# Attention scores over four PSUM banks, the last product of a step split around three down products, and later first values, in a fused attention and feed-forward kernel

## The chip, the cores and the metric

The kernel runs on one core of one Trainium2 chip. The metric is the device time of one execution in microseconds (us): the median of three timed runs was 1604.03 us before the change (1603.75, 1604.03 and 1604.44). A core has a matrix engine (PE, whose matmuls write to PSUM, a memory of eight banks of 512 float32 columns by 128 partitions), a vector engine (DVE), a scalar engine (ACT), GpSimd (POOL), and SyncE (SP), which here only issues transfers. Every engine works through its own list of instructions in order, and engines wait for each other through semaphores.

## The reference

```python
g = sigmoid((x * gate_w).sum(-1))
a = attention(x, wq, wk, wv, wo, beta)         # 32 heads of 18, four segments of 512 tokens
b = (gelu(x @ w_gate) * (x @ w_up)) @ w_down   # 576 -> 4608 -> 576
return g * a + (1 - g) * b

# attention, for each head and segment s, with a memory M, z carried from segment to segment:
p   = softmax(q @ k.T * scale + causal_mask)   # 512 x 512
o   = sigmoid(beta) * (phi(q) @ M) / (phi(q) @ z + 1e-6) + (1 - sigmoid(beta)) * (p @ v)
M  += phi(k).T @ v;   z += phi(k).sum()
```

The sequence has 2048 tokens of width 576. All inputs are float32. The kernel keeps float32 accuracy with float16 matmuls: each operand is split into a high and a low float16 word, and three products (high·high, high·low, low·high) are summed in PSUM.

## The kernel before, in words

A first stage (to about 227 us) projects queries, keys and values and builds the memory term. The stage that the change touches follows: 72 **steps** (`step(v)`, v = 0 to 71), one for each pair of a slice of 128 hidden columns (f = v // 2) and a half of the tokens. A step does three kinds of work, interleaved in an order that the program writes out by hand for PE, ACT, DVE and POOL; only SP's list is ordered by the build.

- **Gate and up.** Gate and up products of two token blocks are formed from seven sub-products of six 512-column matmuls each (`product`), plus single matmuls for the last 64 rows (`rest`, `low_rests`). They accumulate in the PSUM banks V, G (called X in the code) and U (called Y). DVE copies or adds between them: L1138 copies the first sum out of V, L1141 copies G to U, L1177 copies U out, L1196 and L1203 (the g1 and g0 additions) add U and V to what was copied, ACT applies GELU, and at the beginning of the next step `end_pair` runs L1021 (`hidden`), which multiplies by the up product in G and in U. The sub-product named S4 is the last one of a step and adds to U, which the g1 addition must have read before.
- **Down.** From step 4 on, eight down products a step (`down`: six 288-column matmuls, L999) go to the two PSUM banks `dn`, in turn, and DVE adds each to the accumulator (L1007, the eviction). Five of them are called early (`early`, spread over the step), three late.
- **Attention.** From step 2 to 65 two score blocks a step, an even one in the middle and an odd one at the end. `scores` issues four matmuls, one for each block of 128 queries, with 128, 256, 384 and 512 keys (causal). They use 54 rows of the array, either from row 0 or from row 64, and two that lie in different row halves run side by side. DVE adds the mask and takes the maximum of each piece (L910, one custom instruction and a tiny read of its accumulator; `put` in `step`), which also frees the bank. ACT forms exponentials and a float16 pair, POOL the low word, SP transposes it by DMA (L940), and one step later `values` (L954, 40 matmuls of 37 columns for a head's block pair, 20 for each block) multiplies by v into the bank `pv`; `normalize` reads it.

A step of steady state lasts 18.4 to 18.5 us. Steps 0 to 3 have no down products; the first heads' values are issued at the end of steps 3 and 4 (`values(2 * k - 2)` for v <= 4) and at the beginning of steps 4 and 5. From step 69 on, `finish` also splits the output projection's weights: L108 on ACT, L111 on DVE. Behind step 71 come the last down products and the output projection.

Of the kernel before, what the change touches and what calls it, by code (L numbers as in the profile page):

```python
# [13 lines left out]
OP = mybir.AluOpType  # L14
# [4 lines left out]
P = 128  # L19
# [3 lines left out]
DH = 18  # L23
L = 512
# [18 lines left out]
def kernel(ctx: ExitStack, tc: tile.TileContext, xs, wqk, wv, wo, wgu, wd, beta, out):  # L43
# [803 lines left out]
    with tc.tile_pool(name="keep", bufs=2, side="right", reuse_waits="tile") as kp, ExitStack() as tail:  # L847
# [40 lines left out]
        PIECES = (((3,), 0), ((2, 0), 64), ((1,), 0))  # L888

        def scores(a):  # L890
# [6 lines left out]
            for qis, r in PIECES:  # L897
                o = bank("dn", 2) if qis == (1,) else bank("st", 2)
                spots, off, h = [], 0, slice(r, r + 3 * DH)
                for qi in qis:  # L900
                    n = (qi + 1) * P
                    pe.matmul(o[:, off : off + n], q[h, e * L + qi * P : e * L + (qi + 1) * P],  # L902
                              kt[h, e * L : e * L + n], start=True, stop=True)
                    spots.append((qi, o[:, off : off + n]))
                    off += n
                put.append(spots)

            def piece(i):
                for qi, ov in put[i]:
                    dve.tensor_tensor_reduce(prob[a][:, COL[qi] : COL[qi + 1]], ov, mask[:, L - (qi + 1) * P :],  # L910
                                             1.0, -3e38, OP.add, OP.max, mx[a][:, qi : qi + 1])
# [122 lines left out]
        def product(o, f, a, x, h, l, start=False):  # L1034

            w = pair_g[f]
            for k in range(2):
# [72 lines left out]
        def end_pair():  # L1110

            for g in ends:
                hidden(*g)
            for f, c, o, g in ends:
                hidden_pair(f, c, g)
            ends.clear()

        def step(v):
# [19 lines left out]
            dve.tensor_copy(g1, V)  # L1138
# [11 lines left out]
            put(2 * k - 1, 2)  # L1150
            puts.pop(2 * k - 1, None)
            if on(k - 2):
                values(2 * k - 3)
# [31 lines left out]
            if on(k - 2):  # L1185
# [8 lines left out]
            if on(k):  # L1194
                puts[2 * k] = scores(2 * k)
# [152 lines left out]
```

## Time and profile before

| | |
|---|---|
| median of three runs | 1604.03 us (1603.75 to 1604.44) |
| the profiled execution's own time | 1603.76 us |
| its span from the first to the last instruction | 1602.0 us |
| PE busy | 1593.6 us, 99% of the span |
| DVE, ACT, POOL busy | 71%, 73%, 71% |
| granted PE clock | full speed in all slices |
| PE's waits that the trace lists, all entries together | 5.0 us |

A row of a timeline gives start, duration, engine, source line, operation, the program's names of output and inputs, shape, how many instructions are merged in it, and in brackets the idle time of the engine ahead of it with what ended it. A matmul's duration includes the time in which its result drains, so the next one starts well before its end: six 512-column matmuls in a row start 0.215 us apart while each is listed with 0.379 us. An idle time in brackets is counted from the listed end, so it is some 0.16 us shorter than the delay of the start. Times per step are read from the starts.

### The profile page before, as it was taken

How to read it: one execution, taken by the hardware profiler on the slowest of the kernel's cores; microseconds unless marked ns; L12 is line 12 of the kernel's file. 1: busy time of each engine (PE TensorE's matmuls, PEld its weight loads, DVE VectorE, ACT ScalarE, POOL GpSimd, SP SyncE). 2: the span in 40 equal slices, each digit the busy share in tenths (PEclk: the TensorE clock that was granted, in tenths of full speed). 3: DMA queues.
4: the chain of work that ended last, by engine and by line, in shares of the span. 5: the costliest groups of instructions: out<-in, count | busy, mean ns of one | idle time of the engine just before them, and what ended most of it. 6: DMA issues, size and time to landing. Idle time of an engine off the chain costs nothing.

```text
span 1602.0 us, 32613 instructions
## 1 busy us (share of the span) xinstructions
PE 1593.6 (99%) x11924; PEld 932.9 (58%) x11924; DVE 1142.2 (71%) x2938; ACT 1162.6 (73%) x1968; POOL 1136.7 (71%) x1093
## 2 busy tenths in 40 slices
PE   9999999999999999999999999999999999999999
PEld 6655754555555555555555555555555555555577
DVE  6575785777777777777777777777777777766643
ACT  6666446888888888888888888888888888864200
POOL 2233647898878888888979788888879797785300
PEclk9999999999999999999999999999999999999999
DMA  6532344788879788878887897988788788846251
GB/s 246 189 123 80 135 145 99 118 136 124 144 114 143 124 141 123 145 135 126 142 128 132 130 144 125 143 128 143 133 136 137 133 135 128 128 74 154 61 133 60
DMA packets 472016, 209.00 MB, mean 130 GB/s; under 512 B 427568, under 2 KB 437040, under 8 KB 471344
## 3 DMA queue, kind: packets, MB, share of 16 engines
q1 hardware_dynamic: 471856, 206.92, 70.9%
q8 instruction: 94, 1.54, 0.4%
q14 instruction: 66, 0.54, 0.1%
HBM read 90.99 MB, written 27.26 MB: 74 GB/s over the span
## 4 chain that ended last, share of the span: by engine, by line
PE 94%; ACT 2%; DMA 1%; DVE 1%; SPq 1%; issue 0%; DVEq 0%
PE dn L999 26%; PE U L1039 17%; PE V L1039 12%; PE G L1039 11%; PE pv L954 4%; PE st L328 3%; PE st L318 2%; PE U L1046 2%; PE dn L328 2%; PE st L902 2%; PE G L318 1%; PE V L1051 1%; PE G L1051 1%; PE U L318 1%; PE V L1046 1%; PE G L1046 1%
## 5 line engine op out<-in xcount | busy, mean ns | idle before, releaser
L934 POOL TENSOR_TENSOR ph<-pf,ph 128x512 f16<-128x512 f32 (+1 forms) x256 | 354.3, 1406 | 176.6 <-ACT ph L933 176.6
L999 PE MATMUL dn<-paird,hh 128*128 128x288 f16 x3396 | 476.5, 286 | 0.3 <-DVE acc L1007 0.3
L1039 PEld LDWEIGHTS <-pairg 128*128 128x128 f16 x3024 | 285.0, 98 | 308.7 <-issue 13.2
L999 PEld LDWEIGHTS <-hh 128*128 128x128 f16 x3456 | 332.3, 98 | 137.8 <-issue 2.3
L1007 DVE SCALAR_TENSOR_TENSOR acc<-dn,ev,acc 128x288 f32<-128x288 f32 x534 | 274.0, 516 | 94.4 <-PE dn L999 85.6
L923 ACT ACTIVATE pf<-pf,mb,esc 128x512 f32<-128x512 f32 (+3 forms) x512 | 293.0, 642 | 6.7
L1039 PE MATMUL G<-x,pairg 128*128 128x512 f16 x864 | 209.9, 379 | 0.3 <-DVE gl L1021 0.3
L1039 PE MATMUL U<-xt,pairg 128*128 128x512 f16 x864 | 210.0, 379 | 0.0
L1026 POOL TENSOR_TENSOR hh<-gl,hh 128x512 f16<-128x512 f32 x144 | 164.0, 1161 | 45.0 <-ACT hh L1025 45.0
L910 DVE CUSTOM_DVE_ANT_0 pf<-st,mask 128x512 f32<-128x512 f32 (+2 forms) x384 | 184.0, 505 | 0.0
L299 POOL TENSOR_TENSOR pairg<-raw,pairg 128x640 f16<-128x640 f32 (+2 forms) x144 | 174.1, 1231 | 12.3 <-ACT pairg L295 12.3
L933 ACT ACTIVATE ph<-pf 128x512 f16<-128x512 f32 (+1 forms) x256 | 172.4, 720 | 0.0
L1177 DVE COPY gl<-U 128x512 f32<-128x512 f32 x72 | 49.8, 691 | 130.2 <-PE U L1039 130.2
L295 ACT ACTIVATE pairg<-raw 128x640 f16<-128x640 f32 (+2 forms) x144 | 89.5, 648 | 68.4 <-POOL raw L289 38.9
L264 POOL TENSOR_SCALAR raw<-raw,sc 128x640 f32<-128x640 f32 x72 | 135.0, 1888 | 0.0
L1029 ACT ACTIVATE gl<-gl,sc 128x512 f32<-128x512 f32 x144 | 98.2, 717 | 42.4 <-DVE gl L1196 25.0
L1196 DVE TENSOR_TENSOR gl<-U,gl 128x512 f32<-128x512 f32 x72 | 49.8, 691 | 79.9 <-PE U L1051 72.6
L1039 PE MATMUL V<-xt,pairg 128*128 128x512 f16 x432 | 105.7, 381 | 0.0
L1039 PE MATMUL U<-x,pairg 128*128 128x512 f16 x432 | 105.0, 379 | 0.4 <-DVE gl L1196 0.4
L1039 PE MATMUL V<-x,pairg 128*128 128x512 f16 x432 | 104.8, 378 | 0.4 <-ACT hh L1025 0.2
L1025 ACT ACTIVATE hh<-gl 128x512 f16<-128x512 f32 x144 | 82.9, 616 | 26.2 <-DVE gl L1021 26.0
L920 ACT ACTIVATE mb<-mx,esc 128x4 f32<-128x4 f32 x128 | 37.8, 295 | 85.6 <-DVE mx L910 83.0
(268 smaller groups left out, 2569.9 us busy)
## 6 DMA issues: line engine op xcount, KB each, us to landing
raw<-in_wgu_dram SPq DMA_DIRECT2D x36, 640.0 KB
rawd<-in_wd_dram SPq DMA_DIRECT2D x36, 288.0 KB
qk<-stage SPq DMA_DIRECT2D x36, 256.0 KB
qt<-qk SPq DMA_DIRECT2D x128, 72.0 KB
kt<-qk SPq DMA_DIRECT2D x128, 72.0 KB
vp<-vstage SPq DMA_DIRECT2D x16, 296.0 KB
vt<-vp SPq DMA_DIRECT2D x16, 296.0 KB
qt<-qk SPq DMA_DIRECT2D x128, 36.0 KB
```

The source lines that it names most:

```text
L264: pool.tensor_scalar(r, r, scl[f // 2][0][:, 0:1], None, OP.mult)
L295: act.activation(spot(f, *p, 0), raw_g[f][:, p[0] : p[1]], AF.Copy)
L299: pool.tensor_tensor(spot(f, *p, 1), raw_g[f][:, p[0] : p[1]], spot(f, *p, 0), OP.subtract)
L910: dve.tensor_tensor_reduce(prob[a][:, COL[qi] : COL[qi + 1]], ov, mask[:, L - (qi + 1) * P :], 1.0, -3e38, OP.add, OP.max, mx[a][:, qi : q ...
L923: act.activation(r, r, AF.Exp, bias=b[:, qi : qi + 1], scale=esc[:, 0, c : c + 1])
L933: act.activation(h[:, 0, cols], p[:, cols], AF.Copy)
L934: pool.tensor_tensor(h[:, 1, cols], p[:, cols], h[:, 0, cols], OP.subtract)
L999: pe.matmul(o[:, :NH], hh[:, a, q * P : (q + 1) * P], w[:, b, n * NH : (n + 1) * NH], start=i == 0, stop=i == 5)
L1007: dve.scalar_tensor_tensor(av, o[:, :NH], ev, av, OP.mult, OP.add)
L1026: pool.tensor_tensor(hh[:, 1], t, hh[:, 0], OP.subtract)
L1029: act.activation(t, o, AF.Gelu_apprx_tanh, scale=scl[f // 2][0][:, 2 + c : 3 + c])
L1039: pe.matmul(o, w[:, i, (a + k) * P : (a + k + 1) * P], x[:, b + k], start=start and k == 0 and i == 0 and b == h, stop=k == 1 and i == 1, ...
```

## The change

The four score matmuls are issued in the order 512, 384, 256, 128 keys instead of 512, 384, 128, 256, with the row halves as before (0, 64, 64, 0), so the 256-key block moves to the second half and the 128-key block to the first. The 128-key block no longer shares the 384-key block's bank: it takes a `dn` bank, so a score block holds both `st` banks and both `dn` banks.

The DVE work on the pieces moves with it. Of an even block, the two pieces in `dn` come directly behind the scores, ahead of the two additions g1 and g0; the two in `st` stay between evictions. Of an odd block, the pieces in `dn` come between the two `hidden` of the next step, and the two in `st` keep their place.

S4 is issued in two halves of three matmuls, with the three late downs between them. The rest of G (U4) moves from behind product A12 to behind the values in the middle of the step. In steps 4 and 5 values are issued half a step later: blocks 0 and 1 at the beginning and in the middle of step 4, 2 and 3 at the beginning of step 5, 4 in its middle. `normalize(0)` moves to the end of step 4. In steps 1 to 3 the copy out of V comes ahead of `end_pair`. The split of the output weights moves behind the place of `normalize`.

```diff
-        PIECES = (((3,), 0), ((2, 0), 64), ((1,), 0))
+        PIECES = ((3, 0), (2, 64), (1, 64), (0, 0))
...
-            for qis, r in PIECES:
-                o = bank("dn", 2) if qis == (1,) else bank("st", 2)
...
+            for i, (qi, r) in enumerate(PIECES):
+                h, n = slice(r, r + 3 * DH), (qi + 1) * P
+                o = bank("st" if i < 2 else "dn", 2)[:, :n]
...
-        def product(o, f, a, x, h, l, start=False):
+        def product(o, f, a, x, h, l, start=False, ks=(0, 1)):
...
-        def end_pair():
+        def end_pair(between=()):
-            for g in ends:
+            for i, g in enumerate(ends):
                 hidden(*g)
+                if i == 0:
+                    for put in between:
+                        put()
...
+            first, middle = {3: ((), ()), 4: ((0,), (1,)), 5: ((2, 3), (4,))}.get(
+                v, ((2 * k - 3,) * on(k - 2), (2 * k - 2,) * on(k - 1)))
-            end_pair()
-            act_squares(v)
-            V = ahead.pop(v) if v in ahead else first_product(v)
-            g1 = gl_tile()
-            dve.tensor_copy(g1, V)
+            if v in ahead:
+                V, g1 = ahead.pop(v), gl_tile()
+                dve.tensor_copy(g1, V)
+                end_pair()
+                act_squares(v)
+            else:
+                end_pair([lambda i=i: put(2 * k - 1, i) for i in (2, 3)])
+                act_squares(v)
+                V, g1 = first_product(v), gl_tile()
+                dve.tensor_copy(g1, V)
...
-            if on(k - 2):
-                values(2 * k - 3)
+            for a in first:
+                values(a)
...
+            if v >= LAST + 2:
+                finish_pairs(v - LAST)
             product(X, f, A12, x1, 2, 6)
-            rest(X, f, U4, x1, (0,) if fb else (0, 1))
+            if not fb:
+                rest(X, f, U4, x1)
...
             if on(k):
                 puts[2 * k] = scores(2 * k)
+            put(2 * k, 2)
+            put(2 * k, 3)
             dve.tensor_tensor(g1, Y, g1, OP.add)
             gelu(f, e, g1, g1)
-            put(2 * k, 2)
...
-            if on(k - 1) and v > 4:
-                values(2 * k - 2)
+            for a in middle:
+                values(a)
+            if fb:
+                rest(X, f, U4, x1, (0,))
...
-            product(Y, f, S4, x2_, 2, 6)
-            rest(Y, f, UG, x2_, (0,) if fb else (0, 1))
+            product(Y, f, S4, x2_, 2, 6, ks=(0,))
             some(fb - 1, late[:1])
             if low is not None:
                 result_low(low)
             some(fb - 1, late[1:])
-            if on(k - 1) and v <= 4:
-                values(2 * k - 2)
+            if v == 4:
+                normalize(0)
+            product(Y, f, S4, x2_, 2, 6, ks=(1,))
+            rest(Y, f, UG, x2_, (0,) if fb else (0, 1))
```

No instruction is added or removed on PE, DVE, ACT or POOL; they move. In the lists of the changed kernel the lines have other numbers: L900 is the score matmul (L902 before), L906 the mask and maximum (L910), L1003 the eviction (L1007), L1017 `hidden` (L1021), L1144 the copy out of V (L1138), L1147 the copy of G to U (L1141), L1209 and L1215 the g1 and g0 additions (L1196 and L1203).

The first place is PE's list at a score block, here the four score matmuls and the first matmul behind an odd block. Before:

```order
L902 LDWEIGHTS qt
L902 MATMUL st<-kt,qt 128x512
L902 LDWEIGHTS qt
L902 MATMUL st<-kt,qt 128x384
L902 LDWEIGHTS qt
L902 MATMUL st<-kt,qt 128x128
L902 LDWEIGHTS qt
L902 MATMUL dn<-kt,qt 128x256
```

And of the change:

```order
L900 LDWEIGHTS qt
L900 MATMUL st<-kt,qt 128x512
L900 LDWEIGHTS qt
L900 MATMUL st<-kt,qt 128x384
L900 LDWEIGHTS qt
L900 MATMUL dn<-kt,qt 128x256
L900 LDWEIGHTS qt
L900 MATMUL dn<-kt,qt 128x128
```

The third matmul is now the 256-key one, in row half 64 behind the 384-key one, and the fourth is the 128-key one, in row half 0 behind the 512-key one; both go to `dn`.

The second place is DVE's list from the even scores of a step to its first late down, whose eviction is the row that follows in both. Before:

```order
L1196 TENSOR_TENSOR gl<-U,gl 128x512
L910 ISA pf,mx<-dn,mask 128x256
L910 ISA mx 128x1
L1203 TENSOR_TENSOR gl<-V,gl 128x512
L1007 SCALAR_TENSOR_TENSOR acc<-dn,ev,acc 128x288
L910 ISA pf,mx<-st,mask 128x512
L910 ISA mx 128x1
L1007 SCALAR_TENSOR_TENSOR acc<-dn,ev,acc 128x288
L910 ISA pf,mx<-st,mask 128x384
L910 ISA mx 128x1
L910 ISA pf,mx<-st,mask 128x128
L910 ISA mx 128x1
```

Of the change:

```order
L906 ISA pf,mx<-dn,mask 128x256
L906 ISA mx 128x1
L906 ISA pf,mx<-dn,mask 128x128
L906 ISA mx 128x1
L1209 TENSOR_TENSOR gl<-U,gl 128x512
L1215 TENSOR_TENSOR gl<-V,gl 128x512
L1003 SCALAR_TENSOR_TENSOR acc<-dn,ev,acc 128x288
L906 ISA pf,mx<-st,mask 128x512
L906 ISA mx 128x1
L1003 SCALAR_TENSOR_TENSOR acc<-dn,ev,acc 128x288
L906 ISA pf,mx<-st,mask 128x384
L906 ISA mx 128x1
```

Both pieces in `dn` now stand ahead of the two additions, and the list begins with an instruction that waits for the scores, where it began with one that waits for U.

The third place is DVE's list at the border of two steps, from the first `hidden` to the copy of G to U. Before:

```order
L1021 SCALAR_TENSOR_TENSOR gl<-G,sc,gl 128x512
L1021 SCALAR_TENSOR_TENSOR gl<-U,sc,gl 128x512
L1138 COPY gl<-V 128x512
L910 ISA pf,mx<-st,mask 128x512
L910 ISA mx 128x1
L1141 COPY U<-G 128x512
```

And of the change:

```order
L1017 SCALAR_TENSOR_TENSOR gl<-G,sc,gl 128x512
L906 ISA pf,mx<-dn,mask 128x256
L906 ISA mx 128x1
L906 ISA pf,mx<-dn,mask 128x128
L906 ISA mx 128x1
L1017 SCALAR_TENSOR_TENSOR gl<-U,sc,gl 128x512
L1144 COPY gl<-V 128x512
L906 ISA pf,mx<-st,mask 128x512
L906 ISA mx 128x1
L1147 COPY U<-G 128x512
```

The two pieces in `dn` have moved in behind the first `hidden`, so the second one, the copy out of V and the copy of G to U stand behind two more instructions.

More of the change, by code (lines that the diff above doesn't have):

```diff
@@ L1032, in gl_tile @@
             return mp2.tile([P, L], F32, name="gl", bufs=3)
-        def product(o, f, a, x, h, l, start=False):
+        def product(o, f, a, x, h, l, start=False, ks=(0, 1)):
             w = pair_g[f]
-            for k in range(2):
+            for k in ks:
                 for i, b in ((0, h), (0, l), (1, h)):
@@ L1149, in step @@
             put(2 * k - 1, 1)
[L1150 removed]
+            if v < 4:
+                put(2 * k - 1, 2)
+                put(2 * k - 1, 3)
             puts.pop(2 * k - 1, None)
[L1152 to L1153 removed]
+            for a in first:
+                values(a)
             weights_first(fb, i4)
```

20 lines of the change are left out of this document (8 added, 12 removed).

## The prediction

> **What bounds the kernel now.** I read the page first, for the engine that is never idle, then the chain that ended last, then the timelines of PE and DVE through a step of the steady state, then PE's rows that carry an idle time.
>
> ```profile
> PE 1593.6 (99%) x11924; PEld 932.9 (58%) x11924; DVE 1142.2 (71%) x2938; ACT 1162.6 (73%) x1968; POOL 1136.7 (71%) x1093
> PE 94%; ACT 2%; DMA 1%; DVE 1%; SPq 1%; issue 0%; DVEq 0%
> ```
>
> PE works through 99% of the span and carries 94% of the chain. So time comes out only where PE's matmuls get shorter or run side by side, or where one of its few waits goes; and a wait of PE that is new costs its full length. One step (its middle to its end), on PE:
>
> ```profile
> 802.72 0.38 PE L1046 MATMUL U<-x,pairg 128*128 128x512 f16 x1
> 803.03 0.39 PE L1051 MATMUL U<-x,pairg 64*128 64x512 f16 x1
> 803.25 0.38 PE L902 MATMUL st<-kt,qt 54*128 54x512 f16 x3
> 803.48 0.27 PE L902 MATMUL dn<-kt,qt 54*128 54x256 f16 x1
> 803.67 0.67 PE L954 MATMUL pv<-vt,pt 128*128 128x37 f16 x20
> 804.19 1.63 PE L999 MATMUL dn<-paird,hh 128*128 128x288 f16 x12
> 805.66 1.46 PE L1039 MATMUL U<-x,pairg 128*128 128x512 f16 x6
> 806.95 0.38 PE L1046 MATMUL U<-x,pairg 128*128 128x512 f16 x1
> 807.17 2.40 PE L999 MATMUL dn<-paird,hh 128*128 128x288 f16 x18
> 809.50 0.39 PE L1051 MATMUL G<-x,pairg 64*128 64x512 f16 x1
> ```
>
> By the starts: a score block takes 0.42, values 0.52, a down product 0.735 (1.47 for two), a sub-product of six 1.29, a single 512-column matmul 0.22, and a change from 128 rows to 64 adds 0.09 (0.31 instead of 0.22). Three late downs take 2.33 - 0.09 = 2.24 where 3 x 0.735 = 2.20: PE waits some 0.04 in the third, which takes the bank of the first. DVE in the same stretch:
>
> ```profile
> 803.46 0.69 DVE L1196 TENSOR_TENSOR gl<-U,gl 128x512 f32<-128x512 f32 x1 [1.32 <-PE U L1051]
> 804.07 0.41 DVE L910 CUSTOM_DVE_ANT_0 pf<-dn,mask 128x256 f32<-128x256 f32 x1
> 804.41 0.69 DVE L1203 TENSOR_TENSOR gl<-V,gl 128x512 f32<-128x512 f32 x1
> 805.12 0.52 DVE L1007 SCALAR_TENSOR_TENSOR acc<-dn,ev,acc 128x288 f32<-128x288 f32 x1
> 805.56 0.68 DVE L910 CUSTOM_DVE_ANT_0 pf<-st,mask 128x512 f32<-128x512 f32 x1
> 806.16 0.51 DVE L1007 SCALAR_TENSOR_TENSOR acc<-dn,ev,acc 128x288 f32<-128x288 f32 x1
> 806.60 0.54 DVE L910 CUSTOM_DVE_ANT_0 pf<-st,mask 128x384 f32<-128x384 f32 x1
> 807.07 0.28 DVE L910 CUSTOM_DVE_ANT_0 pf<-st,mask 128x128 f32<-128x128 f32 x1
> 807.28 0.08 DVE L910 DVE_READ_ACCUMULATOR2_ANT mx<- 128x1 f32 x1
> 808.10 0.52 DVE L1007 SCALAR_TENSOR_TENSOR acc<-dn,ev,acc 128x288 f32<-128x288 f32 x1 [0.74 <-PE dn L999]
> ```
>
> The last row is the eviction of the first late down: it ends at 808.62, and the third late down starts at 809.50 - 0.09 - 0.735 = 808.67, so the release of a bank reaches PE 0.05 after the eviction's end. DVE had waited 0.74 before it, so the wait of 0.04 is the bare turn-round of two banks.
>
> **Part 1, the score block: shorter.** The pieces by shape:
>
> ```profile
> L902 PE MATMUL st<-kt,qt 54*128 54x384 f16 x128 | 41.5, 325 | 0.0
> L902 PE MATMUL dn<-kt,qt 54*128 54x256 f16 x128 | 34.2, 267 | 0.0
> L902 PE MATMUL st<-kt,qt 54*128 54x128 f16 x128 | 27.3, 213 | 0.0
> ```
>
> 128 columns more cost 0.054 (267 against 213 ns). Row half 0 now streams 512 + 256 columns and half 64 streams 384 + 128, that is 768 against 512; after the change both stream 640. The block ends up to 128 columns = 0.054 earlier; bounds 0 (the halves do not overlap in the second pair) and 0.054. The last piece starts 0.23 after the first, which is one 512-column stream (0.22), so the halves overlap now; I take 0.05. Each step of 62 (4 to 65) has two blocks: -0.10 a step.
>
> **Part 2, what that meets: DVE ahead of the third late down.** S4 is halved, so the late downs start 0.65 + 0.22 earlier; U4 (0.22) now lies before the early ones. Counted from the start s of the even scores, the first late down starts at 0.37 + 0.52 + 0.215 + 1.47 + 0.645 = s+3.22, and the third, with its old wait, at 3.22 + 1.51 = s+4.73.
>
> DVE's list now begins with the 256-key piece. That matmul starts when the 384-key one has streamed, 325 - 213 + 54 = 0.166 after s, and ends 0.267 later, at s+0.44. After it come, start to start: 0.34 (256-key piece), 0.21 (128), g1, g0, 0.44 (eviction), 0.60 (512), 0.44, 0.47 (384), then the eviction of the first late down (0.52) and 0.05. g1 followed by g0, and g0 by an eviction that need not wait, stand in a step without scores:
>
> ```profile
> 1463.69 0.69 DVE L1196 TENSOR_TENSOR gl<-U,gl 128x512 f32<-128x512 f32 x1 [1.32 <-PE U L1051]
> 1464.30 0.68 DVE L1203 TENSOR_TENSOR gl<-V,gl 128x512 f32<-128x512 f32 x1
> 1464.89 0.94 DVE L1007 SCALAR_TENSOR_TENSOR acc<-dn,ev,acc 128x288 f32<-128x288 f32 x2
> ```
>
> 0.61 and 0.59. The sum is 4.27. How long the custom instruction takes to start once its matmul has ended is not in the trace, since it never waits. The nearest rows: an addition starts 0.04 after (803.03 + 0.39 = 803.42, then 803.46), a copy 0.10 after:
>
> ```profile
> 810.15 1.47 PE L1039 MATMUL V<-xt,pairg 128*128 128x512 f16 x6
> 811.72 0.69 DVE L1138 COPY gl<-V 128x512 f32<-128x512 f32 x1 [0.21 <-PE V L1039]
> ```
>
> With 0.04 the third late down starts at 0.44 + 0.04 + 4.27 = s+4.75, some 0.02 to 0.03 later than with its old wait; with 0.10 it is 0.08 to 0.09. I take 0.04, since additions are the commoner kind of the two and the piece, like them, combines two operands: +0.03 a step. The second late down (s+3.96) needs the eviction before the 384-key piece, which starts 0.44 + 0.47 before the first late down's and so releases at s+3.84: no wait. S4's first half (s+2.58) needs g1 read by 0.48 + 0.55 + 0.69 + 0.05 = s+1.77: covered by 0.8; without that cover each 0.1 would cost 6 us.
>
> At the step's border the two pieces delay the second `hidden`, the copy out of V and the copy of G to U by 0.55. The last is needed by the next product into U, which PE reaches only after a down (0.735), values (0.52) and seven matmuls (1.51): 2.8 for 0.70 of copy, so it costs nothing, and the odd block's exponentials start earlier. Steady state: 62 x (-0.10 + 0.03) = **-4.3 us**; bounds -6.2 (no added wait) and -0.6 (0.09).
>
> **Part 3, the first steps.** PE's rows with a wait there:
>
> ```profile
> 240.99 1.47 PE L1039 MATMUL V<-x,pairg 128*128 128x512 f16 x6 [0.22 <-ACT hh L1025]
> 252.17 1.45 PE L1039 MATMUL V<-x,pairg 128*128 128x512 f16 x6 [0.21 <-DVE gl L1138]
> 270.60 0.39 PE L902 MATMUL st<-kt,qt 54*128 54x512 f16 x3
> 271.44 1.46 PE L1039 MATMUL U<-x,pairg 128*128 128x512 f16 x6 [0.35 <-DVE gl L1196]
> 273.62 0.19 PE L954 MATMUL pv<-vt,pt 128*128 128x37 f16 x1 [0.29 <-DMA pt<-ph]
> 274.72 0.64 PE L954 MATMUL pv<-vt,pt 128*128 128x37 f16 x19 [0.91 <-DMA pt<-ph]
> 280.07 0.64 PE L954 MATMUL pv<-vt,pt 128*128 128x37 f16 x19 [0.82 <-DMA pt<-ph]
> ```
>
> Each gap plus 0.16 of drain (379 listed, 215 between starts) is the delay of the start. The copy out of V in front frees V for its second product: -0.38 - 0.37 = -0.75. Block 0's values would now start behind S4, its two single matmuls, a score block, two sub-products and a down, at about 277, and had their last transpose by 274.72; block 1's, in the middle of step 4, are later still than the 280.07 of the row: -0.45 - 1.07 - 0.98 = -2.50. Against that, steps 2 and 3 have no downs between scores and S4, so the g1 addition, now behind two pieces, holds S4 until s+1.77: in step 3 that is 0.93 later than the 271.44 - 270.60 = 0.84 of the row, in step 2, where a product of 1.29 lies between, 0.10. Sum -2.2, bounds -3.2 (the pieces cost nothing) and -0.7 (block 0's waits stay).
>
> **Part 4, the last steps.**
>
> ```profile
> 1453.84 1.46 PE L1039 MATMUL G<-x,pairg 128*128 128x512 f16 x6 [0.27 <-DVE gl L1021]
> 1478.39 0.90 PE L999 MATMUL dn<-paird,hh 128*128 128x288 f16 x6 [0.34 <-DVE acc L1007]
> 1474.94 2.36 DVE L111 SCALAR_TENSOR_TENSOR wo<-wor,wsc,wo 128x576 f16<-128x576 f32 x2 [0.23 <-DMA orow<-oa]
> ```
>
> The first wait goes (S4's second half gives DVE 0.86 before `hidden`): -0.43. The second goes too (-0.50), but the same two L111 now stand ahead of the next eviction, whose bank the second down after it wants about 0.7 before: +0.7. Sum -0.2. On SP the vt and oa transfers move behind others; a transposed block was issued at 814.69 + 2.06 and used at 822.16, so I put that at nothing, and up to +2 if a few blocks come late.
>
> **Sum.** -4.3 - 2.2 - 0.2 = -6.7. The profiled execution took 1603.76 (its span 1602.0), 0.3 below the median, so 1597.1 there and **1597.3** for a median. About 0.2% (3.2 us) is what a measurement can tell from no change.
>
> **Rivals.**
> *PE alone sets the pace:* DVE keeps up, nothing is added: -6.2 - 2.4 = 1595.4. For it: DVE is 71% busy. Against: the sum above leaves no slack.
> *Eviction eats the gain:* the custom instruction starts like a copy, +0.09 a step, so 62 x -0.01 - 2.4 = -3.0, 1601.0. [...]
> *Slower, DVE behind by more:* if the list from the 256-key piece to the eviction takes d longer than 4.27 (pieces in a row may each wait for their bank), every 0.1 costs 6.2; the total is slower than before from d = 0.11. At d = 0.2: +12.4 - 6.7 = 1609.7. For it: no row shows two pieces from `dn` in a row behind scores; against: each link of the sum is a measured one.
> *The second pair does not overlap* as 256 beside 128: the 128-key piece waits until the 256-key one has streamed, the block stays at 0.42, nothing is gained in the steady state and DVE is in time: -2.4, 1601.4. For it: only the starts of two of the four pieces can be read. Against: 128 beside 512 overlaps now.
>
> **Chances.** Forecast 0.40 (its own range 1595.5 to 1599.5), PE alone 0.20, eviction 0.15, slower 0.12, no overlap 0.13. Faster by over 0.2% holds the first two and less than half of the third: 0.65; the rest of the third and the last are within 0.2%: 0.25; slower 0.10. The range takes in the bounds of the parts: 1594.3 to 1603.8.
>
> **What would show it.** Right: score to next start 0.37 in both blocks; late downs 2.26 to 2.28 long, marked as waiting for the eviction if at all; no wait of values before 300 us; a wait for the g1 addition near 272 of 1.3 instead of 0.35. Wrong: score blocks at 0.42; a wait at late downs of 0.1 and more; a wait at S4 or at values in every step.

## The result, and the profile after the change

The changed kernel takes 1599.11 us (median of 7 runs, 1598.48 to 1600.43) where the kernel before takes 1604.15 (7 runs, 1603.75 to 1604.44): a ratio of 0.9971, 95% interval 0.9959 to 0.9983, so 5.0 us or 0.31% faster. Forecast were 1597.3 and -6.7. The profiled execution took 1599.08 us with a span of 1597.4, against 1603.76 and 1602.0: 4.7 in its time and 4.6 in its span.

Busy time and the chain of waits in the page after the change:

```profile
PE 1587.9 (99%) x11924; PEld 932.2 (58%) x11924; DVE 1120.5 (70%) x2938; ACT 1160.2 (73%) x1968; POOL 1135.1 (71%) x1093
PE 93%; DMA 3%; DVE 2%; ACT 1%; issue 1%; POOL 0%; SPq 0%; DVEq 0%; POOLq 0%; ACTq 0%
```

PE still sets the time. New in the chain are 3% of DMA, where it was 1%. The timeline of PE through a step of the steady state, answering to the first one of the prediction:

```profile
800.40 0.38 PE L900 MATMUL st<-kt,qt 54*128 54x512 f16 x2
800.57 0.27 PE L900 MATMUL dn<-kt,qt 54*128 54x256 f16 x2
800.77 0.67 PE L950 MATMUL pv<-vt,pt 128*128 128x37 f16 x20
802.97 0.81 PE L1035 MATMUL U<-x,pairg 128*128 128x512 f16 x3
803.62 2.42 PE L995 MATMUL dn<-paird,hh 128*128 128x288 f16 x18
805.88 0.81 PE L1035 MATMUL U<-x,pairg 128*128 128x512 f16 x3
807.07 0.38 PE L900 MATMUL st<-kt,qt 54*128 54x512 f16 x2
807.44 1.04 PE L1035 MATMUL V<-xt,pairg 128*128 128x512 f16 x4
818.81 0.38 PE L900 MATMUL st<-kt,qt 54*128 54x512 f16 x2
```

Both score blocks take 0.37 (800.40 to 800.77, 807.07 to 807.44), and the three late downs 2.26 (803.62 to 805.88), 0.02 more than the 2.24 of before. From one even block to the next it is 18.41; before, the next one behind the 803.25 of the prediction's rows stood at 821.74, that is 18.49:

```profile
821.74 0.38 PE L902 MATMUL st<-kt,qt 54*128 54x512 f16 x3
```

DVE in the same step:

```profile
800.89 0.42 DVE L906 CUSTOM_DVE_ANT_0 pf<-dn,mask 128x256 f32<-128x256 f32 x1 [1.57 <-PE dn L900]
801.45 0.69 DVE L1209 TENSOR_TENSOR gl<-U,gl 128x512 f32<-128x512 f32 x1
804.58 0.52 DVE L1003 SCALAR_TENSOR_TENSOR acc<-dn,ev,acc 128x288 f32<-128x288 f32 x1
```

The custom instruction starts 0.05 after its matmul's end (800.57 + 0.27 = 800.84), from then on DVE is never idle, and the eviction of the first late down stands at s+4.18 with s = 800.40, as the list of the prediction had it: 0.44 + 0.04 + 4.27 less the eviction's own 0.52 and the 0.05 of its release.

PE's waits in this stage of the changed kernel, as the trace lists them (us in total, times, longest; waits under 0.15 are left out):

```profile
PE pv L950 <- DMA pt<-ph: 1.9, 3, 1.2
PE U L1035 <- DVE gl L1209: 1.4, 1, 1.4
PE dn L995 <- DVE acc L1003: 0.4, 1, 0.4
```

The second is the g1 addition of step 3, the third the L111 ahead of an eviction at 1476 us; both were forecast. The first was not: values that wait for their transposes in the middle of the program. The largest, on PE, and what SP issued ahead of it:

```profile
652.77 0.19 PE L950 MATMUL pv<-vt,pt 128*128 128x37 f16 x1
654.17 0.64 PE L950 MATMUL pv<-vt,pt 128*128 128x37 f16 x19 [1.21 <-DMA pt<-ph]
```

```profile
641.33 0.35 SPq L202 DMA_DIRECT2D rawd<-in_wd_dram  x1
641.73 0.43 SPq L878 DMA_DIRECT2D vt<-vp  x1
642.25 0.73 SPq L867 DMA_DIRECT2D qt<-qk  x1
...
643.52 0.62 SPq L869 DMA_DIRECT2D kt<-qk  x1
644.24 5.57 SPq L936 DMA_TRANSPOSE pt<-ph  x2
```

The two transposes take 5.57 us to issue and end at 649.81. With one small load ahead two take 2.90, as in step 4:

```profile
288.19 2.90 SPq L936 DMA_TRANSPOSE pt<-ph  x2
```

The build has put the load of values (`vt`) between the weights and the queries, 2.5 us ahead of an even block's transposes; before the change it stood directly ahead of the odd block before it, whose pair has more time until its use (637.36 to 648.00, against 647.28 to 656.54 for the even one), and the even pair took 4.37:

```profile
636.87 0.40 SPq L878 DMA_DIRECT2D vt<-vp  x1
...
644.75 0.34 SPq L202 DMA_DIRECT2D rawd<-in_wd_dram  x1
645.19 0.64 SPq L867 DMA_DIRECT2D qt<-qk  x1
...
647.28 4.37 SPq L940 DMA_TRANSPOSE pt<-ph  x2
```

The load of values now stands ahead of fourteen even blocks, one in four steps (10, 18, ..., 114). On average their pair is issued 8.5 us ahead of its use where it was 9.4, holds SP for 5.3 where it held it for 4.8, and is through 3.1 us ahead of the use instead of 4.6. Two of the fourteen come too late in this profile (blocks 42 and 82).

The account, by the difference of the two traces step by step, at the start of PE's first product of each step. A step n of this account and of the comparisons below ends where `step(n)` begins, so it is mostly the work of `step(n - 1)`:

| part | forecast | profiled |
|---|---|---|
| steady state, 62 steps | -4.3 | -5.04 (-0.081 each) |
| first steps (1 to 6, less the steady part of two) | -2.2 | -2.04 |
| last steps (67 to 71) | -0.2 | -0.13 |
| values or scores that wait in steps 22, 25, 31, 45 and 46 | 0, up to +2 | +2.78 |
| ahead of the stage, untouched by the change | | -0.23 |
| sum | -6.7 | -4.66 |

Of the 2.78, 1.94 fell on the two blocks with the load of values ahead (steps 25 and 45), 0.56 on two even blocks without it (22 and 31), and 0.28 on even scores in step 46 that wait for an eviction.

### The profile page after: what moved, and what is told of

Its sections match the earlier page's. It is cut to its first block, busy times and chain, and to the rows that moved or that the text cites. A ratio compares the mean times of both kernels' runs of the same rounds, so it can differ in the third digit from the quotient of the medians.

```text
span 1597.4 us, 32571 instructions
## 1 busy us (share of the span) xinstructions
PE 1587.9 (99%) x11924; PEld 932.2 (58%) x11924; DVE 1120.5 (70%) x2938; ACT 1160.2 (73%) x1968; POOL 1135.1 (71%) x1093
## 4 chain that ended last, share of the span: by engine, by line
PE 93%; DMA 3%; DVE 2%; ACT 1%; issue 1%; POOL 0%; SPq 0%; DVEq 0%; POOLq 0%; ACTq 0%
PE dn L995 24%; PE U L1035 16%; PE V L1035 11%; PE G L1035 11%; PE pv L950 4%; PE st L328 3%; PE st L318 3%; PE dn L328 2%; PE G L318 2%; PE U L1042 2%; DMA pt<-ph 1%; PE U L318 1%; PE G L1047 1%; PE V L1047 1%; PE st L900 1%; PE G L1042 1%
## 5 line engine op out<-in xcount | busy, mean ns | idle before, releaser
L995 PEld LDWEIGHTS <-hh 128*128 128x128 f16 x3456 | 337.2, 98 | 145.9 <-issue 1.4
L1003 DVE SCALAR_TENSOR_TENSOR acc<-dn,ev,acc 128x288 f32<-128x288 f32 x534 | 272.9, 514 | 37.5 <-PE dn L995 36.4
L906 DVE CUSTOM_DVE_ANT_0 pf<-st,mask 128x512 f32<-128x512 f32 (+1 forms) x256 | 157.1, 614 | 0.0
L906 DVE CUSTOM_DVE_ANT_0 pf<-dn,mask 128x256 f32<-128x256 f32 (+1 forms) x256 | 80.7, 353 | 83.2 <-PE dn L900 80.8
L1035 PE MATMUL U<-x,pairg 128*128 128x512 f16 x432 | 116.1, 379 | 1.4 <-DVE gl L1209 1.4
L1021 ACT ACTIVATE hh<-gl 128x512 f16<-128x512 f32 x144 | 83.3, 621 | 25.6 <-DVE gl L1017 25.5
L950 PEld LDWEIGHTS <-pt 128*128 128x128 f16 x2560 | 78.4, 96 | 22.4 <-issue 17.0
```

Source lines behind the costliest of these rows:

```text
L950: pe.matmul(ov, pr[:, 10 * i + COL[qi] // P + kb], v[:, 4 * e + kb, c0 : c0 + VC], start=kb == 0 and i == 0, stop=kb == qi and i == 1)
L995: pe.matmul(o[:, :NH], hh[:, a, q * P : (q + 1) * P], w[:, b, n * NH : (n + 1) * NH], start=i == 0, stop=i == 5)
L1003: dve.scalar_tensor_tensor(av, o[:, :NH], ev, av, OP.mult, OP.add)
L1035: pe.matmul(o, w[:, i, (a + k) * P : (a + k + 1) * P], x[:, b + k], start=start and k == 0 and i == 0 and b == h, stop=k == 1 and i == 1, ...
```

## The experiments

All edits are to the changed kernel, and gains and losses are against its 1599.11. Ratios are to the kernel before, timed on the same chip beside each (1604.04 to 1604.29). Differences of steps compare the profile of a run with that of the changed kernel.

### Old sizes of the two halves

```diff
-        PIECES = ((3, 0), (2, 64), (1, 64), (0, 0))
+        PIECES = ((3, 0), (2, 64), (0, 64), (1, 0))
```

> The changed kernel with one thing undone: the score matmuls run in the old order 512, 384, 128, 256 keys (row halves 0, 64, 64, 0), still over four banks. Theory of the prediction (the two halves stream 768 against 512 columns again): a score block takes 0.42 instead of 0.37, two blocks a step, +0.10; the late downs start 0.05 later against the list of DVE, whose first two pieces now end about 0.07 sooner, so the third late down is back at the bare turn-round of its banks, -0.024. Together +0.076 a step, 62 steps: +4.7 us, so about 1603.8 and a ratio of 1.000 to the kernel before. Rival (the gain of the steady state comes from the moved U4 and the divided S4, not from the sizes): 1599, a ratio of 0.997.

Measured 1606.43, ratio 1.0015 (1.0006 to 1.0023). Of the steps 5 to 65 most are longer by 0.073 to 0.093, median 0.081, where 0.076 was expected. The other 2.4 us sit in single steps, mainly every fourth one from step 34 on with 0.3 to 0.5; in step 50, for one, the 256-key piece, now the last of the four, waits for an eviction that stands behind the arithmetic of the weights' scales on DVE:

```profile
1118.45 0.27 PE L900 MATMUL dn<-kt,qt 54*128 54x256 f16 x1 [0.23 <-DVE acc L1003]
```

So the sizes are worth all of the steady state's gain, and the order of the pieces some more. With four banks but the old sizes the kernel is slower than before.

### S4 in one piece

```diff
-            product(Y, f, S4, x2_, 2, 6, ks=(0,))
+            product(Y, f, S4, x2_, 2, 6)
+            rest(Y, f, UG, x2_, (0,) if fb else (0, 1))
             some(fb - 1, late[:1])
...
-            product(Y, f, S4, x2_, 2, 6, ks=(1,))
-            rest(Y, f, UG, x2_, (0,) if fb else (0, 1))
```

> The changed kernel with S4 in one piece, its rest of U behind it, both ahead of the three late downs (as in the kernel before); only the 64-row matmuls stand between the late downs and the odd scores. Theory: the divided S4 is what pays for scores in four banks. The 128-key piece takes the bank of the third late down, whose eviction releases it 1.50 after that down's start, while PE reaches the piece after 0.735 + 0.31 + 0.22 = 1.27: a wait of 0.23 in every odd score block, less the 0.024 that the third late down no longer waits for DVE: +0.2 a step, 62 steps: +12.8, about 1612. Rival (S4 is divided for nothing but the end of the program, DVE has time enough): -0.024 x 62 = -1.5 and +0.4 for the wait in the last steps, about 1598.

Measured 1615.35, ratio 1.0068 (1.0056 to 1.0081). The steps are longer by 0.20 to 0.21, every fourth by 0.28 and some others by 0.40. The end of an odd score block on PE, and the eviction it waits for on DVE:

```profile
834.52 0.38 PE L900 MATMUL st<-kt,qt 54*128 54x512 f16 x2
834.70 0.49 PE L900 MATMUL dn<-kt,qt 54*128 54x256 f16 x2
835.12 1.47 PE L1035 MATMUL V<-xt,pairg 128*128 128x512 f16 x6
```

```profile
834.40 0.52 DVE L1003 SCALAR_TENSOR_TENSOR acc<-dn,ev,acc 128x288 f32<-128x288 f32 x1 [0.25 <-PE dn L995]
```

The block takes 0.60 instead of 0.37: its second `dn` piece starts only when the eviction of the third late down has ended (834.92). The mechanism is the expected one, the total is 3.4 more. Dividing S4 is what makes four banks for the scores payable.

### U4 in its old place

```diff
-            if not fb:
-                rest(X, f, U4, x1)
+            rest(X, f, U4, x1, (0,) if fb else (0, 1))
             some(fb - 1, early[2:3])
...
-            if fb:
-                rest(X, f, U4, x1, (0,))
             some(fb - 1, early[3:4])
```

> The changed kernel with the rest of G (U4, 0.22) back ahead of the third early down, so ahead of the even scores. Theory (DVE's list, begun by the first piece behind the even scores, sets the start of the third late down at s+4.75): the work ahead of the third late down shrinks by 0.22 and the wait there grows from 0.06 to 0.28 in every step with scores, +0.22 a step, 62 steps: +13 us, about 1612. Rival (PE alone sets the pace and a matmul may stand anywhere): no change, 1599.

Measured 1610.71, ratio 1.0042 (1.0028 to 1.0056). Nearly every step with scores is longer by 0.210 to 0.222, steps 67 to 71 by nothing. The late downs now take 2.40 instead of 2.26, so 0.14 of the 0.22 stands where it was expected:

```profile
808.94 2.56 PE L995 MATMUL dn<-paird,hh 128*128 128x288 f16 x18
811.34 0.81 PE L1035 MATMUL U<-x,pairg 128*128 128x512 f16 x3
```

The other 0.08 stands ahead of the early down behind the values. A matmul of 0.22 that only changes its place costs its full length, since behind the even scores DVE's list is the longer one. The total is 1.7 less than 62 x 0.215 = 13.3; with the slower steps values wait only 0.5 us for transposes, not 1.9, and that is about the difference.

### SP's list in the program's order, loads behind the odd transposes

```diff
                 turn_rows(2 * k - 1)
+                load_head(k + 1)
+            if i4 == 1 and fb:
+                load_v(fb)
...
-            load_head(k + 2)
-            if i4 == 0:
-                load_v(fb)
+            if v < 2:
+                load_head(k + 2)
+            if v == 0:
+                load_v(0)
...
-        with tc.manual_schedule(engines=ORDERED):
+        with tc.manual_schedule(engines=ORDERED | {mybir.EngineType.SP}):
```

> The changed kernel with the transfers' list on SP in the program's order in this stage, the loads of the next head's queries and keys and of values and memory terms placed behind the transposes of the odd block instead of at the end of a step, so that no load is issued right ahead of the transposes of an even block but the weights'. Theory (the changed kernel loses about 2.5 us where values wait for transposes whose issue was stretched to 2.6 to 4.1 us behind loads, in steps 20, 22, 25, 31, 45): those waits go, 1596.6, and the runs scatter less (before 0.7 us, changed 2 us). Rival (the waits are of the transposes themselves and come anyway): 1599. Other side: a list that waits in the program's order holds transposes back behind a weight load that waits for its buffer: values wait in every fourth step, +0.5 each or 1608.

Measured 1699.17, ratio 1.0593 (1.0578 to 1.0607). The other side, and ten times its size. Values wait 62.7 us in 45 places; the large losses stand in every fourth step (9, 13, 17, ...). ACT's waits name the first cause:

```profile
ACT junk L85 <- DMA raw<-in_wgu_dram: 83.6, 15, 7.2
```

Eight loads and the loads of values and memory terms now lie ahead of the weights; ACT's squares wait for these, in order ahead of the exponentials, and so the transposes come late. The second cause is the clock, 0.983 on average in this profile where the changed kernel had 1.000. Eight us of it with one such wait (columns: busy time and number of instructions of PE, of PE's weight loads, of DVE, ACT and POOL; then the granted clock, the DMA share and GB/s):

```profile
362.00:364.00 2.00, 0.19 (x1) 0.10 (x1) 1.75 (x6) 1.31 (x2) 2.00 (x3) 1.00 1.13 254
364.00:366.00 2.00, 1.25 (x23) 0.99 (x24) 0.00 (x0) 1.83 (x3) 2.00 (x2) 0.89 0.95 184
366.00:368.00 2.00, 2.00 (x11) 1.22 (x9) 0.96 (x2) 0.00 (x0) 1.58 (x2) 0.50 0.82 71
368.00:370.00 2.00, 2.00 (x12) 1.16 (x11) 1.15 (x5) 0.48 (x2) 0.00 (x0) 0.76 0.55 113
```

PE was busy 1.44 of the 4 us to 366 and then ran at half its clock: the twelve matmuls of two downs take 2.78 from start to start (365.45 to 368.23) where 1.47 is usual. By the mean clock at most 0.017 x 1697.4 = 29 us were lost so in this profile, an estimate that takes PE as busy in all of the slow time.

### First values in their old places

```diff
-            first, middle = {3: ((), ()), 4: ((0,), (1,)), 5: ((2, 3), (4,))}.get(
-                v, ((2 * k - 3,) * on(k - 2), (2 * k - 2,) * on(k - 1)))
+            first, middle = (2 * k - 3,) * on(k - 2), (2 * k - 2,) * (on(k - 1) and v > 4)
...
-            if v == 4:
-                normalize(0)
+            if on(k - 1) and v <= 4:
+                values(2 * k - 2)
```

> The changed kernel with the first values in their old places: block 0 at the end of step 3, block 1 at the beginning and 2 at the end of step 4, 3 at the beginning and 4 in the middle of step 5 (normalize as before). Theory: the three waits for transposes between 273 and 280 us return, 0.45 + 1.07 + 0.98 = 2.5, less 0.2 since the wait for the g1 addition in step 3 now gives the first of them more time: +2.3, about 1601.4. Rival (the time saved there comes back behind it, since DVE or the transposes set the end of step 5 anyway): 1599.

Measured 1604.58, ratio 1.0007 (0.9999 to 1.0016): +5.5 to the changed kernel where +2.3 was expected. The end of step 3:

```profile
271.74 0.81 PE L1035 MATMUL U<-x,pairg 128*128 128x512 f16 x3 [1.45 <-DVE gl L1208]
274.60 0.19 PE L950 MATMUL pv<-vt,pt 128*128 128x37 f16 x1 [2.06 <-DMA pt<-ph]
275.71 0.78 PE L950 MATMUL pv<-vt,pt 128*128 128x37 f16 x19 [0.91 <-DMA pt<-ph]
276.33 1.44 PE L1035 MATMUL U<-x,pairg 128*128 128x512 f16 x3
277.57 1.06 PE L1042 MATMUL U<-x,pairg 128*128 128x512 f16 x2
```

```profile
268.89:272.30 3.41, 1.96 (x12) 0.69 (x10) 1.86 (x8) 3.39 (x6) 3.01 (x4) 1.00 1.37 84
272.30:275.71 3.41, 0.44 (x4) 0.10 (x2) 1.22 (x3) 3.11 (x6) 1.95 (x2) 1.00 0.79 173
275.71:279.12 3.41, 3.41 (x28) 1.30 (x28) 0.39 (x1) 3.40 (x6) 0.47 (x1) 0.50 0.94 128
```

Two things were missed. Block 0's two transposes, begun at the same 267.55, end their issue 1.0 later than in the kernel before (273.57 against 272.60), behind the same loads in the same order, so the order does not explain this part; and PE, with the V copies saved, comes 0.8 earlier, so the wait of 0.29 became 2.06. And behind three waits in 5.5 us the granted clock is 0.50 from 275.71 to 279.12: three matmuls of S4 take 1.24 from start to start (276.33 to 277.57) where 0.65 is usual. Step 4 of this comparison is longer by 5.26: 2.06 + 0.91 of waits with 0.16 of drain each make 3.29; the slow clock 1.45 (S4's half 0.59, the two singles 0.47, the scores 0.26, values 0.13); the rest, 0.52, are the values that moved into it.

### The pieces behind the g1 addition in the first steps

```diff
-            put(2 * k, 2)
-            put(2 * k, 3)
+            if fb:
+                put(2 * k, 2)
+                put(2 * k, 3)
             dve.tensor_tensor(g1, Y, g1, OP.add)
             gelu(f, e, g1, g1)
+            if not fb:
+                put(2 * k, 2)
+                put(2 * k, 3)
```

> The changed kernel with the two even pieces in the score block's dn banks behind the g1 addition in steps 2 and 3, in front of it from step 4 on. Theory: in step 3 S4 waits 1.45 (listed) for that addition; with the pieces behind it, it waits 0.35 as before the change: -1.1 there, -0.1 in step 2, the pieces and with them the transposes of blocks 0 and 2 come 0.6 later where values have over 3 us to spare: 1598.0. Rival: something else holds S4 there, 1599.

Measured 1599.10, ratio 0.9965 (0.9951 to 0.9979): the changed kernel's time. In the profile the wait for g1 is 0.4 instead of 1.4 and steps 3 to 6 together are shorter by 1.20, as expected. In this profile the gain is lost elsewhere: in steps 17, 37 and 57 values wait that did not wait before (+0.88, +0.91, +0.63), 2.8 us in five places over the program, and the stage ahead, which no edit touches, ends 0.6 later (227.44 against 226.85).

### The rest of U ahead of the late downs

```diff
             product(Y, f, S4, x2_, 2, 6, ks=(0,))
+            rest(Y, f, UG, x2_, (0,) if fb else (0, 1))
             some(fb - 1, late[:1])
...
             product(Y, f, S4, x2_, 2, 6, ks=(1,))
-            rest(Y, f, UG, x2_, (0,) if fb else (0, 1))
```

> The changed kernel with S4's first half followed by the rest of U (0.22) ahead of the late downs; behind them the second half and the 64-row matmuls. Theory (the third late down waits 0.062, of which 0.038 is the turn-round of two banks and 0.024 is DVE's list): 0.22 more work ahead of it leaves 0.038, -0.024 in each of 62 steps: -1.5, about 1597.6; the odd scores' second dn bank is released 1.50 after the third late down's start and wanted 0.735 + 0.65 + 0.31 + 0.22 = 1.91 after it, so it still comes in time. Rival (all of 0.062 is the turn-round): no change, 1599. Other side (the shorter cover in front of the odd scores doesn't do): +0.1 a step, 1605.

Measured 1599.19, ratio 0.9968 (0.9955 to 0.9980). The late downs take 2.24, as before the change:

```profile
803.03 2.40 PE L995 MATMUL dn<-paird,hh 128*128 128x288 f16 x18
805.27 0.81 PE L1035 MATMUL U<-x,pairg 128*128 128x512 f16 x3
```

The steps are shorter by 0.01 to 0.03, most by 0.02, so the 0.024 of DVE's list was real and goes; again the median does not move, with +0.38, +0.49 and +0.24 in steps 37, 45 and 57, where values wait, and 0.5 in the stage ahead.

### SP's list in order, queries and keys behind the even transposes

```diff
             weights_load(fb, i4)
+            if i4 == 1 and fb:
+                load_v(fb)
...
-            if i4 == 0:
-                load_v(fb)
+            if v == 0:
+                load_v(0)
...
-        with tc.manual_schedule(engines=ORDERED):
+        with tc.manual_schedule(engines=ORDERED | {mybir.EngineType.SP}):
```

> As the run with SP's list in the program's order, but with the weights' loads directly behind the transposes of an odd block, the loads of values and memory terms behind them, and the next head's queries and keys behind the transposes of an even block, at the end of the step as in the changed kernel. Theory (the 95 us of the first version come from weights that arrive late: ACT waited 83.6 us for them in its squares, ahead of the exponentials; and the late values of the changed kernel come from loads issued right ahead of an even block's transposes): with the weights early again and only they ahead of the even transposes, neither is left: 1596.6. Rival (any fixed order on SP makes one transfer wait for another's buffer): 1605 or more, with values or ACT's squares waiting.

Measured 1606.72, ratio 1.0016 (1.0007 to 1.0025). The expected part is there: the waits of steps 22, 25, 31 and 45 are gone (-0.40, -1.36, -0.17, -0.58). But odd blocks are now late instead (3, 21, 47, 87 and 101), and block 3 costs 6.2 in step 6: the first steps are short, eight loads stand ahead of its transposes, and behind the waits of 2.02 and 0.86 the clock falls again, to 0.61 on average from 300 to 304 us:

```profile
298.65 0.19 PE L950 MATMUL pv<-vt,pt 128*128 128x37 f16 x1 [2.02 <-DMA pt<-ph]
299.71 0.79 PE L950 MATMUL pv<-vt,pt 128*128 128x37 f16 x19 [0.86 <-DMA pt<-ph]
300.33 2.73 PE L1035 MATMUL V<-x,pairg 128*128 128x512 f16 x6
302.85 0.50 PE L1042 MATMUL V<-x,pairg 128*128 128x512 f16 x1
```

Six matmuls take 2.52 where 1.30 is usual.

### SP's list in order, weights last

```diff
                 turn_rows(2 * k - 1)
+                load_head(k + 1)
...
-            load_head(k + 2)
+            if v < 2:
+                load_head(k + 2)
...
-        with tc.manual_schedule(engines=ORDERED):
+        with tc.manual_schedule(engines=ORDERED | {mybir.EngineType.SP}):
```

> The changed kernel with SP's list in the program's order: transposes of an odd block, then the next head's queries and keys, then the weights' loads, then the transposes of an even block; loads of values and memory terms behind those, at the end of every fourth step. Theory (the values of the changed kernel are late in blocks 18, 26, 36, 42, 54, 66, 82, mostly those of the step in which weights, values, queries and keys are all issued right ahead of the transposes; the first ordered version lost its 95 us in every fourth step, where the loads of values and memory terms lay ahead of the weights): with queries and keys 2 us after a step's even scores and the weights from 6 us on, an even block's transposes at 9.5 us find fewer loads in flight: the 2.5 us of late values go, 1596.6. Rival (wherever the loads stand, they are ahead of some transposes or of weights that ACT waits for): 1604 to 1610.

Measured 1684.42, ratio 1.0504 (1.0490 to 1.0519). The theory of this run fell: it put the end of the odd transposes' issue 2 us behind the even scores, and they end 6.4 behind (348.03 against 341.62). So the weights are issued directly ahead of the even transposes, and ACT waits for them 64.9 us:

```profile
352.71 0.37 SPq L196 DMA_DIRECT2D raw<-in_wgu_dram  x1
...
354.01 8.27 SPq L936 DMA_TRANSPOSE pt<-ph  x3
```

### Three things mended

The two edits of "the pieces behind the g1 addition" and "the rest of U", and the output weights' split in two places:

```diff
-                finish_pairs(v - LAST)
+                finish_pairs(v - LAST, 0)
...
             some(fb - 1, late[1:])
+            if v >= LAST + 2:
+                finish_pairs(v - LAST, 1)
...
-        def finish_pairs(i):
+        def finish_pairs(i, j):
...
-                for k in ((0, 1), (2, 3), (4,))[i - 2]:
+                for k in ((0, 1), (2, 3), (4,))[i - 2][j : j + 1]:
```

> The changed kernel with three things mended, SP's list left to the build: the pieces behind the g1 addition in steps 2 and 3, the rest of U ahead of the late downs, and the split of the output weights (two L111 in steps 69 and 70) one ahead of the additions and one behind the late downs. Theory: -1.2, -0.022 x 62 = -1.4 and -0.7 (the two waits in step 70): 1595.8. Rival (each of the first two was measured alone and moved the median by nothing, since more values came late): 1599.

Measured 1597.38, ratio 0.9958 (0.9945 to 0.9970): 1.7 less than the changed kernel, half of the expected 3.3. Step 70 is shorter by 0.80, steps 3 to 6 by 1.14 and the steady steps by 0.02 as before. In its profile 0.8 of that goes in the stage ahead (227.67 against 226.85), and values wait 2.1 us.

### The three things and the list with weights last

> The three things mended and SP's list in the program's order together. Theory: 1599.1 - 3.3 - 2.5 = 1593.3. Rival (the ordered list only moves the late transposes elsewhere): as the run with the ordered list alone, less 3.3.

Its list on SP is that of "weights last", the other edits those of "three things mended". Measured 1682.36, ratio 1.0492 (1.0477 to 1.0506): the rival, with 2.1 less than that list alone.

### Order on SP and later use together

The three mended things and the list with queries and keys behind the even transposes, with these edits:

```diff
                 turn_rows(2 * k - 1)
+                if v == 4:
+                    load_head(3)
...
-            for a in first:
-                values(a)
             weights_first(fb, i4)
...
+            for a in first:
+                values(a)
             product(Y, f, S2, t, 4, 6)
...
-            for a in middle:
-                values(a)
             if fb:
                 rest(X, f, U4, x1, (0,))
+            for a in middle:
+                values(a)
...
-            load_head(k + 2)
+            if v != 3:
+                load_head(k + 2)
```

> The three things mended together with the list on SP in which the next head's queries and keys follow an even block's transposes, at the end of a step (the ordered version that came out at 1606.7), and with what that one showed to be short: head 3's queries and keys go behind the transposes of block 3 (in step 6 the first-version list lost 6.2 with them in front), the values of an odd block move 1.5 us later, behind product A22 and the rest of V, and U4 goes ahead of the even block's values (0.22 more time for these). Theory (late transposes are a matter of which loads stand ahead of them and of the time that values leave them; both are now given): 1597.4 less the 2.2 of values that wait in the mended kernel: about 1595. Rival (transposes are held up at random by loads, whatever the order): 1597 to 1600. Other side (the values moved between V's rest and S2 delay a product or bring a wait of their own in every step): 1605 and more.

Measured 1595.31 (5 runs, 1594.56 to 1595.87), ratio 0.9943 (0.9929 to 0.9956), the fastest version here: 3.8 less than the changed kernel. What is left of the waits for transposes:

```profile
PE pv L950 <- DMA pt<-ph: 0.4, 2, 0.2
```

It was 2.1 with the three mended things alone, and the time fell by 2.1 (1597.38 to 1595.31). So the transposes' lateness is for the most part a matter of what SP issues ahead of them and of when values are wanted. This run changes both and does not tell them apart; that the order counts for the even blocks is shown by the run with queries and keys behind the even transposes, where their four waits went without a later use.

## Why the prediction was right, and where it was off

The forecast of a faster kernel held, 1.8 us short of its time and inside its own range, by 0.4 us. That it stayed inside is in part luck: the steady state came out 0.7 better than its sum, and a term put at nothing cost 2.8.

**Score block (Part 1).** Right: 0.42 to 0.37 in both blocks, and the run with the old sizes gives back 0.081 a step. The rival in which the second pair does not overlap is excluded.

**DVE ahead of the third late down (Part 2).** Right, in size too: +0.03 forecast, 0.024 found (2.26 against 2.24), the custom instruction's start 0.05 against the 0.04 taken and the bound of 0.10. Two runs change one term of that sum each and moved the steps by what it gives: 0.22 less work ahead costs 0.215 (0.14 of it at the third late down), 0.22 more brings 0.02. The rival "PE alone sets the pace" falls with the first of these; "eviction eats the gain" and "slower" were wrong by size only. What the divided S4 does for the odd scores' banks the prediction did not see: undivided it costs 0.20 a step by another wait, 16 us in all.

**First steps (Part 3).** -2.0 against -2.2; the g1 wait was 1.4 as forecast ("1.3"), values wait nowhere before 300 us. But the move of the first values was priced as if the rest stood still: put back into the changed kernel they cost 5.5, not 2.5. There the issue of block 0's transposes ends 1.0 later (why is open), PE comes 0.8 earlier, and behind the waits PE ran 3.41 us at a granted clock of 0.50.

**Last steps (Part 4).** -0.1 against -0.2. Two old waits go, and the same L111 make new ones at 1476 and 1478 us, as written.

**The term that failed** is the last sentence of Part 4: SP's reordered list "at nothing, and up to +2". It cost 2.8 in this profile, 2.5 of it by values. The prediction took one transposed block, whose issue ended 5.4 us ahead of its use, and that is not one of those with the load of values ahead. The build's new order put that load ahead of the even blocks of every fourth step, and there 3.1 us are left on average and 3.0 in block 42, less than its landing took: PE got it 4.4 us after the issue's end (649.81 to 654.17). The other terms (steady state 0.7 better, the stage ahead 0.2 better, first and last steps 0.2 worse) make up part of it.

Two of the prediction's sums are also off. Its parts' upper bounds add up to 1602.5, or 1604.5 with the +2 for late blocks, not to 1603.8, and the rival without overlap comes to 1601.6, not 1601.4. Neither changes the forecast.

## What to carry to other kernels

Where a slow engine's list decided here, a matmul's place was worth its length: U4, 0.22 long, costs 0.215 a step more ahead of the scores that start DVE's list than between them and the wait for the list's end, and the rest of U, 0.22 long too, brought 0.02 when it moved from behind that wait to ahead of it, which is all that the list still cost. So count, from the event that starts the list, what stands on both sides. When an engine's order is left to the build, a change elsewhere can reorder it, as the load of values moved here from ahead of an odd block to ahead of an even one: read that engine's list through a whole cycle, and judge a transfer by how long its issue takes behind its neighbours (2.90 to 7.33 us for two transposes in the changed kernel), not by its median. Two gains that each bring nothing in the median may still be there, hidden by a later wait: compare step by step before discarding them.

## What the hardware showed that was not expected

**Behind waits close together PE ran at half its clock for about 3.4 us.** The mean granted clock of the changed kernel's profile is 1.000. In the run with the first values in their old places it is 0.50 from 275.71 to 279.12, that is for 3.41 us; in the first ordered list, by the rows above (0.89, 0.50, 0.76), for some 3.4 from 365.6 on. Ahead of each lies a stretch in which PE was little busy: 1.44 of the 4 us to 366 in the ordered list, 1.12 of 4 (296 to 300) in the run with queries and keys behind the even transposes. In the run with the first values in their old places the wait of 1.45 alone left PE busy for 57% of its stretch (1.96 of 3.41), and the clock stayed at 1.00; the two others left 13% (0.44 of 3.41), and the next stretch ran at half. In the changed kernel the single wait of 1.45 did nothing to the clock: 1.00 from 270 to 274 us, with PE busy for 2.55 of the 4, and from 274 to 278. At which busy share the clock falls was not shown. A stretch at half clock cost 1.45 us in the run with the first values in their old places and about the same in step 6 of the run with queries and keys behind the even transposes (1.22 of it on the six matmuls), and, by the estimate above, at most 29 of the 100 us that the first ordered list lost; most of that loss is the waits themselves, of values alone 62.7.

**Two transposes take 2.9 to 7.3 us to issue.** In the changed kernel they hold SP for 2.90 us with one load between them and the transposes before (288.19), and for 3.45 to 7.33 with two and more (1103.71 and 467.32); three take 8.27 behind the weights in the run with weights last (354.01). In the fourteen even blocks above it is 5.3 on average in the changed kernel. Block 42, one of them, took 5.57 there (644.24) and 3.44 in the last run (643.19), where the loads of queries, keys and values stand elsewhere. But block 0 took 5.04 before the change and 6.02 in the run with the first values in their old places, with the same loads ahead, so the order is not all of it. The issue, not only the landing, is what comes late, and what stands behind it on SP comes late with it: the load of keys behind block 42's transposes starts at 649.86, 0.05 after their end.
